# Threshold of eleven score steps moved from VectorE to GpSimd, in four instructions per step

## The chip, the cores and the metric

The kernel runs on one core of a Trainium2 chip. A core has five engines that run their own instruction lists side by side and meet through semaphores: TensorE (PE in the profile, with PEld for its weight loads), VectorE (DVE), ScalarE (ACT), GpSimd (POOL) and SyncE (SP, which here only issues DMAs). The metric is the device time of one execution in microseconds (us); lower is better. Before the change it is 442.55 us, the median of three runs from 441.95 to 442.66.

## What is computed

Eight batches of an attention with a threshold, followed by a gated MLP whose gate mixes the sequence positions. The part that the change touches is the second line of `_attn_ref`: only scores within `tau` (0.02) of the row's largest are kept.

```python
def _attn_ref(q, k, v, tau):                  # q, k, v: (8, 8, 576, 64) float32
    scores = (1.0 / np.sqrt(64)) * np.matmul(q, k.transpose(0, 1, 3, 2))
    thresh = np.max(scores, axis=-1, keepdims=True) - tau
    scores = np.where(scores >= thresh, scores, -1000000000.0)
    scores = scores - np.max(scores, axis=-1, keepdims=True)
    attn = np.exp(scores)
    attn = attn / (np.sum(attn, axis=-1, keepdims=True) + 1e-09)
    return np.matmul(attn, v)

def _moe_ref(x, w_in, w_spatial, b_spatial, w_out):   # x: attention, heads side by side
    h = np.maximum(x @ w_in, 0.0)
    u, v = h[..., :512], h[..., 512:]
    v_n = (v - mean(v)) / np.sqrt(var(v) + 1e-06)     # over the last axis
    v_s = np.einsum('ts,bsd->btd', w_spatial, v_n) + b_spatial[None, :, None]
    return (u * v_s) @ w_out
```

## The kernel before

**Steps.** The attention of one batch is cut into 18 score steps, 144 in all, numbered g = 18b + j. A step is 128 rows of scores of two heads: 128 x 2 x 576 values. `scores` and `scores_end` (the matmuls of line 712) fill one of two PSUM tiles, `s_ring[g % 2]`, so the matmuls of step g+2 wait until ScalarE has read step g out of its tile.

**Two ways to threshold.** `top` (line 746) takes each row's largest score on VectorE. Then a step goes one of two ways, by the table `ON_ACT`:

- On ScalarE (84 steps): `shift` (line 752, VectorE, 128 x 2) makes a bias, `spread` (line 761) subtracts it with a Prelu whose slope throws what is under the threshold to minus infinity, and `exps` (line 781) takes the exponential.
- Through VectorE (60 steps): `spread` (line 764) writes e = exp(score - largest) into one of three tiles, `e_ring[g % 3]`, one ScalarE instruction per head, and `mask` (line 776) makes the numerators p = (e >= ctau) * e in one VectorE instruction of 128 x 1152, where `ctau` is exp(-tau). Both of its tensor inputs are the same tile e in SBUF.

The numerators go to a `p_ring` tile in bfloat16, are transposed by DMA (tokens T) and multiplied with v (tokens P, p).

**The order of the work.** It is written out by hand: `ORDER` holds four lists of tokens, for batches 0, 1, 2 and 3 to 7, and `run_token` emits them one after another; each engine runs its instructions in that order. `name:d` means "of the batch d before this one" (d = -1: the next one). The tokens that matter here:

| token | what it emits | engine, line |
|---|---|---|
| S, Y | the score matmuls of a step, first and last part | PE, 712 |
| G | a GpSimd no-op between them (`turn_bank`): it waits until S has written the bank that both heads share, and Y waits for it | POOL, 727 |
| M (H, K by halves) | the largest of each row | DVE, 746 |
| B | the bias of a step on ScalarE | DVE, 752 |
| E, F | `spread` of head 0 and head 1 | ACT, 761 or 764 |
| Z / W | `exps` / `mask` | ACT, 781 / DVE, 776 |
| sq, sv | q and k, or v, of a pair of heads brought into another layout | POOL, 197 / 224 and 230 |
| QA, QB, QR and qa, qb, qr, kd | transposes of q, k and the last rows on PE, the copies out of PSUM on ACT, and a small copy on POOL (350) | PE, ACT, POOL |
| v, ev, bv, bs | a block of the MLP's v, its Relu (with row sums in ev), its statistics in bs | PE, ACT 554/557, DVE 565 |
| n, k, N | the mean from those sums (`mean`), the squares of v minus that mean (`square`), and the normalized v (`norm`) | POOL 570, ACT 576, POOL 583 to 595 |

A step that is masked by VectorE in batch j is listed as W in `ORDER`; in batches 3 to 7 these are steps 5, 6, 7, 8, 9, 11, 14 and 17. Around steps 7 and 11 the list for those batches reads:

```
F7 M8 v1 sv0 E7 ev0 W7 S9 T10 bv1 G9 Y9 E8 QR3 M9 v2 qr3 F8 kd3 o3 W8 E9 S10 ev2 G10 sq0:-1 TR0 eo3 Y10
P01 F9 M10 n0 P00 sv1 k0 L5:-1 S11 B10 p01 E10 G11 N0 ...
... v4 F11 M12 L2:-1 E11 u1 bv4 B12 W11 S13 eu1 G13 n3 T20 Y13 F12 N1 QR0:-1 M13 R0 qr0:-1 E12 QA0:-1 k2 r0
S14 G14 qa0:-1 B13 N2 bs4 Y14 F13 OUT3 P11 M14 E13 ...
```

In the compiled program the no-op of token G is an instruction of GpSimd's sequencer alone: it waits for a PE semaphore and raises one that PE waits for.

Of the kernel before, what the change touches and what calls it, by code (L numbers as in the profile page):

```python
# [15 lines left out]
ORDER = [(  # L16
    "L7:0 L8:0 S0:0 G0:0 Y0:0 Ci0:0 S1:0 M0:0 G1:0 Y1:0 QB1:0 L9:0 M1:0 F0:0 QA1:0 E0:0 B1:0 qb1:0 W0:0 "
    "S2:0 F1:0 G2:0 Y2:0 E1:0 QR1:0 M2:0 Z1:0 S3:0 G3:0 Y3:0 dqa1:0 E2:0 T00:0 M3:0 qr1:0 F2:0 kd1:0 "
    "sq2:0 S4:0 B3:0 W2:0 F3:0 G4:0 Y4:0 E3:0 Z3:0 M4:0 S5:0 Ci2:0 G5:0 Cis0:0 L3:-1 Y5:0 QR2:0 QA2:0 "
    "B4:0 Cb0:0 dqr2:0 sv2:0 F4:0 M5:0 QB2:0 E4:0 qb2:0 T01:0 dqa2:0 S6:0 F5:0 G6:0 sq3:0 Y6:0 E5:0 M6:0 "  # L20
    "Z4:0 S7:0 G7:0 kd2:0 Y7:0 sv0:0 B6:0 F6:0 RP00:0 M7:0 Ci3:0 RP01:0 Cis2:0 E6:0 Ci1:0 rp01:0 drp00:0 "
    "Z6:0 B7:0 W5:0 QR3:0 S8:0 G8:0 F7:0 sv3:0 Y8:0 T10:0 P00:0 E7:0 dqr3:0 M8:0 sv1:0 Z7:0 S9:0 G9:0 "
    "Y9:0 B8:0 p00:0 F8:0 QB3:0 M9:0 E8:0 R0:0 S10:0 L0:-1 B9:0 r0:0 G10:0 kd3:0 E9:0 Y10:0 Cs2:0 F9:0 "
    "M10:0 L4:-1 Z8:0 S11:0 G11:0 Cis3:0 Y11:0 qb3:0 T11:0 M11:0 E10:0 QA3:0 F10:0 B11:0 qa3:0 S12:0 "
    "E11:0 G12:0 Cis1:0 Y12:0 F11:0 M12:0 L1:-1 Z9:0 S13:0 L6:-1 G13:0 Cbs0:0 Y13:0 B12:0 Z11:0 W10:0 "
    "XR0:0 P10:0 QR0:-1 F12:0 M13:0 E12:0 T20:0 S14:0 dqr0:-1 B13:0 p10:0 G14:0 E13:0 Y14:0 P01:0 F13:0 "
    "M14:0 Z12:0 S15:0 sq0:-1 Cs1:0 p01:0 G15:0 F14:0 Y15:0 L5:-1 Css4:0 XP0:0 M15:0 E14:0 P11:0 Z13:0 "
    "kd0:-1 dxp0:0 p11:0 QA0:-1 T21:0 B15:0 F15:0 QB0:-1 S16:0 E15:0 dqb0:-1 G16:0 W14:0 qa0:-1 Y16:0 "
    "S17:0 Z15:0 G17:0 sq1:-1 Y17:0 M16:0 Cs0:0 P20:0 L7:-1 XP1:0 Css2:0 dxp1:0 L8:-1 B16:0 p20:0 E16:0 "
    "M17:0 Css3:0 F16:0 T30:0 P21:0 F17:0 p21:0 E17:0 Z16:0 L2:-1 L9:-1 "),  # L30
(
    "WS2:1 S0:0 dws2:1 G0:0 Y0:0 S1:0 M0:0 G1:0 Y1:0 QA1:0 M1:0 F0:0 RP11:1 qa1:0 rp11:1 W17:1 QB1:0 E0:0 "
    "RP10:1 F1:0 S2:0 W0:0 E1:0 G2:0 sq2:0 Y2:0 rp10:1 S3:0 M2:0 qb1:0 G3:0 Y3:0 T31:1 sq3:0 QR1:0 P30:1 "
    "B2:0 M3:0 qr1:0 F2:0 QA2:0 kd1:0 E2:0 W1:0 F3:0 S4:0 E3:0 G4:0 Y4:0 p30:1 Z2:0 S5:0 M4:0 Co0:1 G5:0 "
    "Css0:1 Y5:0 qa2:0 L1:-1 XP2:1 M5:0 xp2:1 QB2:0 sv1:0 qb2:0 QR2:0 qr2:0 B4:0 B5:0 R1:1 W3:0 F4:0 "
    "T00:0 P31:1 E4:0 E5:0 r1:1 S6:0 F5:0 G6:0 kd2:0 p31:1 Y6:0 Z4:0 M6:0 XP3:1 WS0:1 S7:0 L0:-1 ws0:1 "
    "G7:0 dxp3:1 Cos0:1 L4:-1 Y7:0 F6:0 Css1:1 v0:1 M7:0 E6:0 v1:1 bv0:1 W6:0 F7:0 v2:1 T01:0 E7:0 bs0:1 "
    "S8:0 bv1:1 G8:0 ev2:1 bs1:1 Y8:0 RP01:0 Z5:0 n2:1 M8:0 QB3:0 sv2:0 Co1:1 S9:0 qb3:0 G9:0 sv0:0 L5:-1 "
    "drp01:0 Y9:0 E8:0 v3:1 M9:0 XR1:1 F8:0 sq0:-1 RP00:0 bv3:1 S10:0 B9:0 drp00:0 E9:0 T10:0 G10:0 N0:1 "
    "W7:0 Y10:0 k2:1 u3:1 F9:0 M10:0 QA3:0 eu3:1 S11:0 qa3:0 G11:0 Y11:0 B10:0 L8:-1 W8:0 F10:0 sq1:-1 "  # L40
    "QR3:0 P00:0 L6:-1 qr3:0 E10:0 u1:1 p00:0 Z9:0 M11:0 S12:0 kd3:0 G12:0 eu1:1 Cos1:1 Y12:0 T11:0 N2:1 "
    "P01:0 E11:0 M12:0 v4:1 F11:0 B12:0 p01:0 S13:0 bv4:1 W11:0 G13:0 F12:0 Y13:0 Co2:1 u0:1 E12:0 L3:-1 "
    "M13:0 Z10:0 QB0:-1 S14:0 eu0:1 dqb0:-1 G14:0 sv3:0 Y14:0 Z12:0 bs3:1 R0:0 T20:0 N1:1 P11:0 B13:0 "
    "r0:0 F13:0 E13:0 p11:0 u4:1 H14:0 WS3:1 N3:1 eu4:1 ws3:1 QA0:-1 K14:0 L7:-1 WS1:1 B14:0 XR0:0 F14:0 "
    "S15:0 dws1:1 Cos2:1 bs4:1 G15:0 qa0:-1 Y15:0 E14:0 M15:0 QR0:-1 WS4:1 qr0:-1 Z14:0 S16:0 T21:0 G16:0 "
    "N4:1 Y16:0 B15:0 dws4:1 E15:0 XP0:0 u2:1 dxp0:0 F15:0 H16:0 P20:0 Z13:0 K16:0 S17:0 L9:-1 eu2:1 "
    "B16:0 G17:0 kd0:-1 p20:0 Y17:0 E16:0 TR1:0 P10:0 H17:0 Z15:0 s0:1 p10:0 K17:0 F16:0 es0:1 E17:0 "
    "P21:0 F17:0 p21:0 T30:0 Z16:0 Co3:1 L2:-1 "),
(
    "S0:0 G0:0 Y0:0 XP1:1 M0:0 QA1:0 xp1:1 S1:0 qa1:0 G1:0 B0:0 Y1:0 E0:0 QR1:0 M1:0 XP2:1 qr1:0 xp2:1 "  # L50
    "s1:2 F0:0 B1:0 W17:1 E1:0 QB1:0 F1:0 S2:0 G2:0 es1:2 qb1:0 T31:1 Y2:0 S3:0 Z0:0 M2:0 G3:0 kd1:0 Y3:0 "
    "sq2:0 s2:2 M3:0 E2:0 Cos3:2 QA2:0 F2:0 sq3:0 L1:-1 es2:2 F3:0 S4:0 L0:-1 W2:0 E3:0 G4:0 Y4:0 L8:-1 "
    "P30:1 qa2:0 M4:0 Z1:0 QB2:0 S5:0 qb2:0 p30:1 T00:0 G5:0 Y5:0 B4:0 W3:0 QR2:0 P31:1 qr2:0 E4:0 kd2:0 "
    "s3:2 F4:0 M5:0 Z4:0 S6:0 p31:1 G6:0 sv0:0 Y6:0 B5:0 es3:2 R1:1 F5:0 sq0:-1 M6:0 E5:0 o0:2 L5:-1 Z5:0 "
    "L6:-1 S7:0 r1:1 G7:0 Y7:0 eo0:2 B6:0 X1:1 o1:2 M7:0 F6:0 E6:0 o2:2 T01:0 deo1:2 E7:0 S8:0 deo2:2 "
    "F7:0 G8:0 sv3:0 Y8:0 Z6:0 S9:0 M8:0 G9:0 Y9:0 u2:1 TR0:0 W7:0 F8:0 v0:1 eu2:1 E8:0 L4:-1 M9:0 QA3:0 "
    "bv0:1 S10:0 qa3:0 G10:0 T10:0 B9:0 bs0:1 Y10:0 E9:0 QR3:0 o3:2 F9:0 dqr3:0 M10:0 s4:2 Z9:0 S11:0 "
    "es4:2 eo3:2 W8:0 G11:0 N0:1 L7:-1 Y11:0 F10:0 v1:1 OUT3:2 E10:0 M11:0 QB3:0 bv1:1 S12:0 qb3:0 G12:0 "
    "B11:0 bs1:1 Y12:0 E11:0 T11:0 sv1:0 v2:1 F11:0 M12:0 N1:1 v3:1 bv2:1 B12:0 u3:1 bs2:1 bv3:1 bs3:1 "
    "u1:1 kd3:0 eu3:1 Z11:0 W10:0 R0:0 OUT1:2 S13:0 L3:-1 eu1:1 r0:0 G13:0 sv2:0 E12:0 Y13:0 v4:1 M13:0 "  # L60
    "F12:0 S14:0 bv4:1 T20:0 B13:0 G14:0 sq1:-1 Y14:0 F13:0 P01:0 M14:0 N2:1 E13:0 P00:0 Z12:0 p01:0 "
    "S15:0 B14:0 G15:0 p00:0 L2:-1 Y15:0 F14:0 QR0:-1 M15:0 QB0:-1 qr0:-1 P10:0 qb0:-1 E14:0 B15:0 bs4:1 "
    "QA0:-1 Z13:0 S16:0 T21:0 p10:0 G16:0 kd0:-1 Y16:0 N3:1 dqa0:-1 F15:0 P20:0 M16:0 E15:0 u4:1 Z15:0 "
    "S17:0 p20:0 G17:0 N4:1 Y17:0 B16:0 OUT4:2 eu4:1 P11:0 Z14:0 TR1:0 u0:1 p11:0 E16:0 H17:0 s0:1 eu0:1 "
    "K17:0 F16:0 T30:0 P21:0 es0:1 F17:0 p21:0 E17:0 Z16:0 X0:0 L9:-1 "),
(
    "S0:0 G0:0 Y0:0 QA1:0 M0:0 QR1:0 S1:0 qr1:0 qa1:0 G1:0 kd1:0 B0:0 Y1:0 W17:1 E0:0 QB1:0 F0:0 s1:2 "
    "M1:0 qb1:0 Z0:0 S2:0 T31:1 G2:0 sq2:0 B1:0 Y2:0 es1:2 E1:0 s3:2 M2:0 F1:0 R1:1 B2:0 es3:2 F2:0 S3:0 "
    "r1:1 G3:0 E2:0 Y3:0 s2:2 L0:-1 Z1:0 M3:0 L3:-1 Z2:0 S4:0 es2:2 G4:0 B3:0 Y4:0 F3:0 o0:2 M4:0 E3:0 "
    "T00:0 P30:1 eo0:2 B4:0 S5:0 E4:0 p30:1 G5:0 F4:0 Y5:0 QA2:0 M5:0 Z3:0 P31:1 L4:-1 qa2:0 S6:0 p31:1 "  # L70
    "F5:0 G6:0 sq3:0 Y6:0 X1:1 E5:0 o1:2 M6:0 o2:2 eo1:2 T01:0 W5:0 F6:0 QB2:0 E6:0 S7:0 eo2:2 G7:0 W6:0 "
    "Y7:0 qb2:0 S8:0 Z4:0 G8:0 Y8:0 M7:0 L1:-1 QR2:0 s4:2 qr2:0 L8:-1 kd2:0 v0:1 sv2:0 es4:2 F7:0 M8:0 "
    "v1:1 sv0:0 E7:0 ev0:1 W7:0 S9:0 T10:0 bv1:1 G9:0 Y9:0 E8:0 QR3:0 M9:0 v2:1 qr3:0 F8:0 kd3:0 o3:2 "
    "W8:0 E9:0 S10:0 ev2:1 G10:0 sq0:-1 TR0:0 eo3:2 Y10:0 P01:0 F9:0 M10:0 n0:1 P00:0 sv1:0 k0:1 L5:-1 "
    "S11:0 B10:0 p01:0 E10:0 G11:0 N0:1 p00:0 Y11:0 F10:0 T11:0 QB3:0 M11:0 v3:1 qb3:0 Z10:0 n2:1 bs1:1 "
# [1048 lines left out]
```

## Time and profile before

| what | value |
|---|---|
| median of three runs | 442.55 us (441.95 to 442.66) |
| span of the profiled execution (first to last instruction) | 440.2 us |
| PE, DVE, ACT, POOL busy | 411.0, 394.3, 388.0, 178.7 us |
| `mask`, line 776 | 60 instructions, 85.5 us, mean 1427 ns |
| `top`, line 746, both heads at once | 135 instructions, 1352 to 1361 ns |
| `spread`, line 764, one head | 120 instructions, mean 749 ns |
| GpSimd `norm`, line 595, 128 x 512, float32 to bfloat16 | 28 instructions, mean 772 ns |
| GpSimd `mean`, line 570, 128 x 1 | 16 instructions, mean 440 ns (some 190 ns where nothing disturbs it) |
| granted TensorE clock | 0.999 |

A batch of the steady part takes some 51 us. Instruction rows in the timeline are given as start, duration, engine, line, operation, tiles; a bracket at the end is idle time of that engine before the instruction and what ended it. An engine's busy share is no more than a first hint: which wait ends last, stage by stage, tells what a change there is worth.

### The profile page before, as it was taken

What the parts mean: (1) busy time and instruction counts of PE and PEld (TensorE: products, weight loads), DVE (VectorE), ACT (ScalarE), POOL (GpSimd) and SP (SyncE); (2) the same over time, 40 slices, a digit from 0 to 9 for tenths busy, and PEclk for the clock granted to TensorE, in tenths of its full rate; (3) what the DMA queues carried; (4) which work ended last, traced back from release to release, by engine and by line L of the source; (5) the groups of instructions that cost most, each with busy time, mean ns of one, the idle gap of its engine ahead of it and who ended that gap; (6) DMA issues with size and microseconds to landing.
All of it is one profiled execution on the core that took longest, in us unless ns stands there. A gap on an engine that the chain in (4) does not pass through costs nothing.

```text
span 440.2 us, 12827 instructions
## 1 busy us (share of the span) xinstructions
PE 411.0 (93%) x4997; PEld 260.9 (59%) x5048; DVE 394.3 (90%) x641; ACT 388.0 (88%) x621; POOL 178.7 (41%) x383
## 2 busy tenths in 40 slices
PE   8677789999999999999999999999999999999995
PEld 4454556566555666666565666666566666565553
DVE  6997899998999898999999998999989998999782
ACT  3899799999899999999999989999899999999352
POOL 1445443860416511773146711574127711345021
PEclk9999999999999999999999999999999999999999
DMA  7999999899999999999999999999999998976913
GB/s 197 284 213 215 286 224 240 176 180 208 247 157 246 189 188 193 223 220 187 234 216 166 246 216 200 221 231 182 218 188 221 235 190 158 163 111 83 281 67 109
DMA packets 222620, 88.15 MB, mean 200 GB/s; under 512 B 193632, under 2 KB 218336, under 8 KB 222560
## 3 DMA queue, kind: packets, MB, share of 16 engines
q1 hardware_dynamic: 222032, 86.48, 95.0%
q8 instruction: 40, 0.66, 0.6%
q0 software_dynamic: 160, 0.52, 0.3%
q10 hardware_dynamic: 368, 0.33, 0.2%
q14 instruction: 20, 0.16, 0.1%
HBM read 32.79 MB, written 9.44 MB: 96 GB/s over the span
## 4 chain that ended last, share of the span: by engine, by line
DVE 36%; PE 35%; ACT 18%; issue 8%; DMA 1%; POOL 0%; POOLq 0%; DVEq 0%; ACTq 0%
PE s L712 14%; DVE s L746 13%; DVE p L776 9%; DVE negm L746 6%; ACT e L761 6%; ACT e L764 4%; ACT p L781 4%; PE f L610 3%; PE f L668 3%; PE f L397 2%; PE f L639 2%; DVE xn L406 2%; PE f L338 2%; DVE st L565 2%; PE f L545 2%
## 5 line engine op out<-in xcount | busy, mean ns | idle before, releaser
L712 PE MATMUL s<-qkT 64*64 64x160 f32 (+1 forms) x2304 | 171.8, 415 | 13.5 <-ACT e L761 7.3
L712 PEld LDWEIGHTS s<-qkT 64*64 64x64 f32 x2304 | 106.7, 132 | 68.4 <-ACT e L761 17.4
L761 ACT ACTIVATE e<-s,negm 128x576 f32<-128x576 f32 x168 | 117.2, 744 | 12.1 <-DVE negm L752 6.5
L746 DVE TENSOR_REDUCE s<-s 128x2 f32<-128x1152 f32 (+1 forms) x91 | 115.3, 1268 | 10.8 <-PE s L712 9.3
L764 ACT ACTIVATE e<-s,negm 128x576 f32<-128x576 f32 x120 | 84.8, 749 | 9.4 <-DVE negm L746 8.1
L746 DVE TENSOR_REDUCE negm<-s 128x2 f32<-128x1152 f32 (+1 forms) x62 | 81.2, 1313 | 8.8 <-PE s L712 8.5
L776 DVE SCALAR_TENSOR_TENSOR p<-e,ctau 128x1152 bf16<-128x1152 f32 x60 | 85.5, 1427 | 1.3 <-ACT e L764 1.2
L781 ACT ACTIVATE p<-e 128x1152 bf16<-128x1152 f32 x68 | 79.0, 1171 | 0.4
L197 POOL COPY qn<-ql 128x512 f32<-128x512 f32 x31 | 25.5, 821 | 81.1 <-PE s L712 80.7
L397 PE MATMUL f<-v,pT 128*128 128x65 bf16 x1008 | 44.5, 194 | 0.0
L397 PEld LDWEIGHTS <-pT 128*128 128x128 bf16 x1024 | 41.4, 97 | 3.5 <-issue 1.8
L350 POOL COPY qkT<-qkT 64x64 f32<-64x64 f32 x32 | 7.9, 247 | 85.3 <-PE s L712 42.4
L406 DVE TENSOR_TENSOR xn<-f,r 128x256 bf16<-128x256 f32 (+1 forms) x93 | 35.4, 380 | 2.9
L639 PE MATMUL f<-wsT,vn 128*128 128x512 bf16 x117 | 32.6, 380 | 1.4 <-ACT qkT L320 0.4
L610 PE MATMUL f<-xT,w_in 128*128 128x512 bf16 x111 | 29.4, 381 | 0.5
L392 PE MATMUL f<-v,pT 128*128 128x130 bf16 x126 | 27.7, 220 | 1.1 <-DVE xT L314 0.7
L595 POOL TENSOR_SCALAR vn<-vrel,rs,nm 128x512 bf16<-128x512 f32 (+1 forms) x35 | 27.0, 770 | 3.6
L320 ACT COPY qkT<-f 128x512 f32<-128x512 f32 (+1 forms) x56 | 24.5, 439 | 3.4 <-PE f L357 3.2
L545 PE MATMUL f<-w_in,xT 128*128 128x512 bf16 x99 | 26.8, 379 | 0.8
L668 PE MATMUL f<-w_o,gT 128*128 128x512 bf16 x92 | 24.2, 380 | 0.4
L224 POOL CAST v<-vl 128x512 bf16<-128x512 f32 x32 | 20.0, 625 | 10.3 <-PE s L712 9.4
L230 POOL CAST v<-vx 64x64 bf16<-64x64 f32 x64 | 20.8, 326 | 1.9
(166 smaller groups left out, 570.9 us busy)
## 6 DMA issues: line engine op xcount, KB each, us to landing
vl<-in_v_dram SPq DMA_DIRECT2D x16, 512.0 KB, 4.7
ql<-in_q_dram SPq DMA_DIRECT2D x15, 512.0 KB, 5.0
kl<-in_k_dram SPq DMA_DIRECT2D x15, 512.0 KB, 5.3
out_dram<-oo SPq DMA_DIRECT2D x12, 512.0 KB, 5.0
uT<-in_moe_w_in_dram SPq DMA_DIRECT2D x3, 512.0 KB, 4.8
uT<-in_moe_w_spatial_dram SPq DMA_DIRECT2D x2, 576.0 KB, 4.6
pT<-p SPq DMA_TRANSPOSE x65, 6.3
vx<-in_v_dram SPq DMA_DIRECT2D x16, 64.0 KB, 3.7
```

The source lines that it names most:

```text
L397: nc.tensor.matmul(out=t[:, at + 65 * h:at + 65 * h + 65], lhsT=pt[:, 5 * h + j, :], rhs=vt[:, 6 * h + j, :], start=False, stop=(h == 1 an ...
L406: nc.vector.tensor_tensor(out=dst, in0=o[ps, g0:g1, 0:64], in1=r[ps, g0:g1].unsqueeze(2).broadcast_to([ps.stop - ps.start, g1 - g0, 64]), ...
L545: nc.tensor.matmul(out=t, lhsT=x_of(b, f, slice(c * P, (c + 1) * P)), rhs=w_in[:, f, 512:1024], start=(f == 0), stop=(f == 3))
L610: nc.tensor.matmul(out=t, lhsT=w_in[:, m, f * P:(f + 1) * P], rhs=x_of(b, m, slice(0, 512)), start=(m == 0), stop=(m == 3))
L639: nc.tensor.matmul(out=t, lhsT=vn[:, c, f * P:(f + 1) * P], rhs=wsT[:, c, 0:512], start=(c == 0), stop=(c == 4))
L668: nc.tensor.matmul(out=t[:n], lhsT=gs[b][:, f, c * P:c * P + n], rhs=w_o[:, f, :], start=(f == 0), stop=(f == 3))
L712: made.append(nc.tensor.matmul(out=s_ring[g % 2][halves[k], at[h] + lo:at[h] + hi], lhsT=qks[n][halves[h], 0, m:m + 64], rhs=qks[n][halves ...
L746: nc.vector.tensor_reduce(out=nm[:, heads], in_=view(s_ring[g % 2], at[h0], dims), axis=AX.X, op=ALU.max, negate=True)
L761: nc.scalar.activation(out=e, in_=s, func=ACT.Prelu, bias=bias_, scale=scale if steps[g][1] == 4 else 1.0, alpha=1e30)
L764: nc.scalar.activation(out=e, in_=s, func=ACT.Exp, bias=bias_)
L776: nc.vector.scalar_tensor_tensor(out=numerators(g), in0=ef, scalar=ctau, in1=ef, op0=ALU.is_ge, op1=ALU.mult)
L781: nc.scalar.activation(out=numerators(g), in_=e_ring[g % 3].rearrange("p h s -> p (h s)"), func=ACT.Exp)
```

## The change

In eleven steps (step 7 of batch 2, steps 7 and 11 of batches 3 to 7) the one VectorE instruction of `mask` is replaced by four GpSimd instructions. Per head, a comparison writes a mask of ones and zeros in bfloat16 into a new tile of its own (128 x 576), and a product of e and that mask writes the numerators. The table `ON_ACT` becomes `WAYS`, a letter per step: `a` for on ScalarE, `w` for `mask` as before, `s` for the new way. The other letters (`n`, `q`) are in the code but in no entry of the table, so `half_step` and `half_e` have no effect here. All other steps keep their way.

```diff
+WAYS = [
+    "wawaawaaaawaaawaaw",
+    "wwawaawwwaawaaaaaw",
+    "aawwaaaswawaaaaaaw",
+    "aaaaawwswwasaawaaw",
+]
...
+    kept_head = [const.tile([P, S], t, name=f"kept{h}")
+                 for h, t in enumerate((BF16, BF16))]
...
+    def keep_head(g, h):
+
+        nc.gpsimd.tensor_scalar(out=kept_head[h], in0=e_ring[g % 3][:, h, :],
+                                scalar1=ctau, scalar2=None, op0=ALU.is_ge)
+
+    def mask_head(g, h):
+
+        nc.gpsimd.tensor_tensor(out=numerators(g)[:, S * h:S * h + S], in0=e_ring[g % 3][:, h, :],
+                                in1=kept_head[h], op=ALU.mult)
...
+    stepwise = {"B": "anq", "Z": "a", "W": "wnq", "I": "sq", "J": "s", "U": "s", "V": "s"}
...
-        if kind in ("B", "Z", "W") and on_act(g) == (kind == "W"):
+        if kind in stepwise and way(g) not in stepwise[kind]:
             return
...
+             "I": lambda g: keep(g) if way(g) == "q" else keep_head(g, 0), "J": lambda g: keep_head(g, 1),
+             "U": lambda g: mask_head(g, 0), "V": lambda g: mask_head(g, 1)}[kind](g)
```

In `ORDER` the token W of these steps becomes four: I and J (the comparisons) stand where W stood, U and V (the products) come later, each behind a token G. The lists are otherwise the same, token for token; they are only wrapped at another width.

```
batch 2, step 7
-  G9 Y9 u2 TR0 W7 F8 v0 eu2 E8 ... S10 qa3 G10 T10 B9
+  G9 Y9 u2 TR0 I7 J7 U7 F8 v0 eu2 E8 ... S10 qa3 G10 V7 T10 B9
batches 3 to 7, step 7
-  E7 ev0 W7 S9 T10 bv1 G9 Y9 ... S10 ev2 G10 sq0:-1 TR0
+  E7 ev0 I7 J7 S9 T10 bv1 G9 U7 Y9 ... S10 ev2 G10 V7 sq0:-1 TR0
batches 3 to 7, step 11
-  bv4 B12 W11 S13 eu1 G13 n3 T20 ... S14 G14 qa0:-1 B13 N2
+  bv4 B12 I11 J11 S13 eu1 G13 U11 n3 T20 ... S14 G14 V11 qa0:-1 B13 N2
```

Counted in the built programs, VectorE loses 11 instructions of line 776 and GpSimd gains 22 comparisons and 22 products; PE, ACT and SP keep their instructions and their order.

## The prediction

> **What bounds the kernel now.** I read the page's busy shares and chain first, then the groups by shape for prices, then the steady part in stretches, and last the timeline around a removed instruction.
>
> ```profile
> PE 411.0 (93%) x4997; PEld 260.9 (59%) x5048; DVE 394.3 (90%) x641; ACT 388.0 (88%) x621; POOL 178.7 (41%) x383
> ...
> DVE 36%; PE 35%; ACT 18%; issue 8%; DMA 1%; POOL 0%; POOLq 0%; DVEq 0%; ACTq 0%
> ```
>
> Three engines are near 90%, and GpSimd, idle for more than half the time, is nowhere on the chain. That invites the change. But a share is a mean; batch 3 in stretches says who sets the pace where:
>
> ```profile
> core 0: us, PE busy (x) PEld busy (x) DVE busy (x) ACT busy (x) POOL busy (x), PEclk, DMA share, GB/s
> 178.00:184.00 6.00, 5.88 (x79) 3.51 (x77) 5.61 (x5) 5.69 (x13) 4.07 (x8) 1.00 1.25 259
> 184.00:196.00 12.00, 11.94 (x161) 7.86 (x162) 11.60 (x21) 11.94 (x24) 9.00 (x19) 1.00 0.93 207
> ```
>
> From 184 to 196 us ScalarE is busy for 11.94 of 12 us, and GpSimd for 9.0: just here it is not idle. Steps 7 and 11 lie at 178 and 190. The timeline around step 7:
>
> ```profile
> 178.52 1.41 DVE L776 SCALAR_TENSOR_TENSOR p<-e,ctau 128x1152 bf16<-128x1152 f32 x1
> ...
> 178.61 1.71 POOL L230 CAST v<-vx 64x64 bf16<-64x64 f32 x2
> ...
> 179.84 1.35 DVE L746 TENSOR_REDUCE negm<-s 128x2 f32<-128x1152 f32 x1
> ...
> 183.53 0.18 POOL L570 TENSOR_SCALAR nmean<-sm 128x1 f32<-128x1 f32 x1
> ...
> 183.74 0.72 ACT L576 ACTIVATE sq<-vrel,nmean 128x512 bf16<-128x512 f32 x1
> ...
> 186.58 0.42 PEld L338 LDWEIGHTS f<-identf,qn 128*128 128x128 f32 x4 [0.30 <-ACT qkT L320]
> ```
>
> Three things are to be seen. The mask of step 7 (178.52) lies beside the matmuls of step 9 (another row of the timeline, 178.53 to 179.73), so the next reduction (179.84) waited for PE as much as for the mask. On GpSimd two copies and a mean of row sums run from 182.38 to 183.71, and ScalarE's square, which needs that mean, starts 0.03 us after it, at 183.74, when ScalarE has just come free (183.67). And behind the square ScalarE has no gap, while PE already waits for it (the copy L320) at 186.58.
>
> **Removed.** Eleven instructions of 1.41 us, 15.5 us of VectorE time; what counts is how much earlier the next reduction can start. Step 7, batches 3 to 7: step 9's scores end at 179.73 and a reduction starts some 0.06 behind them (step 10: 182.85 to 182.91), so 179.79 for 179.84: 0.05. Step 11: its mask runs 190.44 to 191.85 and the next reduction starts at 191.77, while the scores end at 191.46: 0.25. Batch 2: the mask is at 126.91, the next reduction at 128.25, and its scores are done at 126.58, so it can come 1.40 earlier; but the spread that follows (129.89) stands behind a ScalarE copy that ends at 129.79, so 0.15 are left.
>
> **Added: prices.** No row has these operations at this size.
>
> ```profile
> L595 POOL TENSOR_SCALAR vn<-vrel,rs,nm 128x512 bf16<-128x512 f32 x28 | 21.6, 772 | 2.9
> ...
> L224 POOL CAST v<-vl 128x512 bf16<-128x512 f32 x32 | 20.0, 625 | 10.3 <-PE s L712 9.4
> ...
> L244 POOL CAST w_in<-uT 128x1024 bf16<-128x1024 f32 x3 | 3.1, 1040 | 5.3 <-PE s L712 5.3
> ...
> L586 POOL TENSOR_SCALAR rs<-ss 128x1 f32<-128x1 f32 x16 | 3.1, 192 | 4.6 <-ACT pr L781 2.2 <-PE s L712 1.3
> ```
>
> Comparison: L595 is the same kind (float32 to bfloat16, per-partition scalar). 0.19 fixed (L586) and 0.58 for 511 more columns give 0.19 + 0.65 = 0.845 us at 576. Ends: 0.67 (a cast: 0.62 at 512, and 0.42 for 512 more) and 1.04 (the cast of 1024). Product: it reads two inputs. Not under 0.845 (one input) and not over 1.69 (two passes). It reads 2 x 576 elements: L244 extended from 1024 to 1152 gives 1.15, and with the 1.25 by which L595 exceeds a cast of its size, 1.43; I take 1.3. A step thus puts 2 x 0.845 + 2 x 1.3 = 4.3 us on GpSimd for 1.4 taken from VectorE.
>
> [...]
>
> [...] The 64 x 64 cast at 178.61 took 1.41 us instead of 0.23 and ended at 180.02, just after the mask (179.93); in the trace every GpSimd read that overlaps a mask is held so (0.95 us for a mean of 0.19, ending at 191.90 behind a mask ending at 191.85). The other way the mask is held less: one that started 0.55 us before the end of a GpSimd copy (15.60; copy to 16.15) took 1.76, one 0.31 before (87.05) took 1.51, against 1.41. So a mask loses its overlap less some 0.2. L595, which has all kinds of VectorE work beside it, shows no hold by anything but masks: its 28 rows at 128 x 512 all take 771 to 774 ns.
>
> [...]
>
> **Step 7, batches 3 to 6**, in the times of batch 3. Without the mask the cast pair at 178.61 needs 0.53 (the pair at 184.21): to 179.14. Then I 179.22 to 180.07, J to 180.87 (instructions with no wait between them overlap by 0.05, as the two copies do), U 180.82 to 182.12. The mask of step 8 comes at 181.06 into U, loses 1.06 - 0.2 and runs to 183.3; the next reduction slips by 0.3, which is covered by what follows. The small copy (L350) is held by that mask to 183.4. V (allowed since the G at 182.18) runs 183.47 to 184.77, then the two copies, in the queue behind V, to 185.9, the mean to 186.05. The square waits for it: 186.08 instead of 183.74, **2.34 us late**. Behind it ScalarE's queue is full to 196 us: the spreads of step 10 (184.57), the copy at 185.95 for which PE waits at 186.58, and so the scores of step 12 and its reduction. I see no cover, so I count all of it: 4 x 2.34 = 9.4 us. Even with nothing before it late, V alone stands between G10 and the copies: 182.28 + 0.845 + 1.33 is 184.45, 0.7 late.
>
> **Step 7, batch 7.** No next batch, so no two copies: V to 184.77, mean to 184.9, square at 184.94 and the next spread 0.83 later, 185.77 against 184.57: 1.2 us. **Batch 2** has no mean here, and GpSimd is idle from 126.0 to 132.5: the four end by 130.9. Gain 0.15.
>
> **Step 11, five times.** I waits for the spread that ends at 189.92: 190.02 to 190.87, J to 191.66, U to 192.91, a mean to 193.07, the normalization's four instructions (2.15 from mean to end in the trace, 191.90 to 194.05) to 195.22, V 195.17 to 196.47. Spread F14 writes the same e tile (14 and 11 are equal modulo 3) and now must wait for V: 196.54 against 196.34. So 0.2 lost, 5 x 0.2 = 1.0, and the 0.25 of VectorE is not used.
>
> **G.** A sequencer no-op does not wait for the instruction in execution: the one at 150.78 ended inside an L595 that ran 150.26 to 151.03, and at 179.07 one ended while a cast was held to 180.02. So G costs nothing; I waits only for spreads that S waits for too. **DMAs:** T11 now waits for V, 184.8, against its issue at 184.18; its consumer P11 runs at 195. Nothing. SP's later issues slip by 0.6, with microseconds to spare.
>
> **Sum:** 9.4 + 1.2 + 1.0 - 0.15 = +11.4 us. The profiled execution has a span of 440.2, the median is 2.35 above it; I add to the median: 453.9 (span 451.6).
>
> **Ends.** Low: 0.67 and 0.845, hardly a held mask: the square is 1.1 late (4.3 in all), batch 7 nothing, step 11 gains 0.25 x 5, batch 2 up to 1.4: +1.7, 444.2. High: 1.04 and 1.69: the mask of step 8 gets the port before U, V ends at 186.3, the square is 3.9 late (15.6), batch 7 2.8, step 11 1.4 x 5 = 6.9: +25, 467.8.
>
> **Rivals.**
> (a) Faster: VectorE sets the pace. For it: 36% of the chain. Place: the reductions behind the removed masks; price: all that they can move, 1.4 + 5 x 0.05 + 5 x 0.25 = 2.9 us, 439.6. It decides only where the mean comes before ScalarE is free (183.67): copies and mean take 1.33 of the 1.5 us from G10 on, so V would have to fit in 0.2, while the cheapest row says 0.845. Or ScalarE's delay would have to be made up later; its first gaps over 0.2 come at 207. 10%.
> (b) Cheap products, the low end: 443.5 to 447, 9%.
> (c) Dear ones, masks and GpSimd blocking each other in turn: 461 to 469, 8%.
> (d) The no-ops stick behind a full GpSimd queue: G9 then waits for J (180.87 for 179.07), G13 for J (0.9), G14 for the normalization (1.6), so PE stalls 4.3 us more in each of five batches: some 475. The two no-ops above speak against it. 4%.
> (e) The losses and gains cancel: 3%.
> That the change does less than it says is excluded by the instruction counts.
>
> My forecast (447 to 461) has 66%. About 0.2% (0.9 us) is what a measurement of this kernel can tell from no change: faster 10%, same 3%, slower 87%. The range from 443.5 to 464 leaves out (a), (d), (e) and part of (c), 2 in 10.
>
> **What would show it.** On the profile after: a wait of several microseconds of ACT L590 (the square) for POOL in batches 3 to 6, four times over 1.5 us; products between 1.1 and 1.5 us and comparisons near 0.85; masks of step 8 of some 2.2 us; the copies qn, kn directly behind V; F14 waiting for POOL; no wait of PE on the no-op's line. I am wrong if the square doesn't wait, or if it waits and the batches are no longer: then ScalarE was not what set the end there.

## The result, and the profile after

The changed kernel takes 475.35 us (median of four runs, 473.59 to 476.89) against 442.61 us for the kernel before in the same comparison: a ratio of 1.073, 95% interval 1.069 to 1.076. The forecast was 453.9 us, the range 443.5 to 464. The direction was right; the loss is 32.7 us where 11.4 were forecast, and the time lies outside the range. The profiled execution took 474.39 us, span 472.6.

The first page of the profile after, busy shares and the shares of the chain that ended last:

```profile
span 472.6 us, 12892 instructions
...
PE 426.1 (90%) x4997; PEld 263.9 (56%) x5048; DVE 383.2 (81%) x630; ACT 387.7 (82%) x621; POOL 234.4 (50%) x427
...
PE 35%; DVE 22%; ACT 20%; issue 11%; POOL 9%; DMA 1%; POOLq 0%; DVEq 0%; ACTq 0%
```

GpSimd, at 0% of the chain before, is now on 9% of it. VectorE and ScalarE have fallen from 90 and 88% busy to 81 and 82%, PE from 93 to 90%. The same two stretches of batch 3 as before the change show where:

```profile
core 0: us, PE busy (x) PEld busy (x) DVE busy (x) ACT busy (x) POOL busy (x), PEclk, DMA share, GB/s
178.00:184.00 6.00, 4.75 (x39) 2.00 (x37) 3.50 (x3) 5.46 (x12) 5.80 (x6) 1.00 1.22 258
184.00:196.00 12.00, 11.31 (x134) 6.73 (x135) 8.85 (x14) 9.03 (x18) 10.54 (x17) 1.00 0.85 163
```

From 178 to 184 us it is GpSimd that is full (5.80 of 6), and PE is busy for 4.75 instead of 5.88. The groups by shape give the prices that the prediction had to bound:

```profile
L822 POOL TENSOR_SCALAR kept<-e,ctau 128x576 bf16<-128x576 f32 x22 | 37.8, 1724 | 4.3 <-ACT e L793 3.7
L827 POOL TENSOR_TENSOR p<-e,kept 128x576 bf16<-128x576 f32 x22 | 28.6, 1303 | 0.4
```

A product takes 1.30 us, as taken. A comparison takes 1.72, twice what was taken (0.845) and above the upper end (1.04). The waits (engine and line that waited, for whom; us in total, times, longest):

```profile
PEld s L732 <- POOLq L747: 33.4, 24, 2.9
...
PE s L732 <- POOLq L747: 18.7, 15, 2.2
...
ACT sq L590 <- POOL nmean L584: 15.0, 5, 3.2
```

The third row is what the prediction named: the square (L590) waits for the mean, 3.2 us instead of 2.3. The first two are what it excluded: PE waits for the no-op of the G tokens (L747). PEld and PE wait at the same time; PE's wait is shorter (1.21 against 1.93 us at G10 of batch 3, in the timeline below), as its matmuls run to 182.86 and its weight loads end at 182.14. In the kernel before, the first row (there L712 and L727) was 1.8 us in all:

```profile
PEld s L712 <- POOLq L727: 1.8, 4, 0.8
```

The timeline of batch 3 after the change, around steps 7 and 11:

```profile
179.17 3.43 POOL L822 TENSOR_SCALAR kept<-e,ctau 128x576 bf16<-128x576 f32 x2
...
182.57 1.39 POOL L827 TENSOR_TENSOR p<-e,kept 128x576 bf16<-128x576 f32 x1
...
184.02 0.23 POOL L364 COPY qkT<-qkT 64x64 f32<-64x64 f32 x1
184.07 0.19 PEld L732 LDWEIGHTS s<-qkT 64*64 64x64 f32 x4 [1.93 <-POOLq L747]
184.07 0.49 PE L732 MATMUL s<-qkT 64*64 64x160 f32 x4 [1.21 <-POOLq L747]
184.34 1.28 POOL L827 TENSOR_TENSOR p<-e,kept 128x576 bf16<-128x576 f32 x1
...
186.92 0.72 ACT L590 ACTIVATE sq<-vrel,nmean 128x512 bf16<-128x512 f32 x1 [3.21 <-POOL nmean L584]
...
192.96 3.44 POOL L822 TENSOR_SCALAR kept<-e,ctau 128x576 bf16<-128x576 f32 x2 [0.30 <-ACT e L793]
...
196.36 1.28 POOL L827 TENSOR_TENSOR p<-e,kept 128x576 bf16<-128x576 f32 x1
...
198.83 0.26 POOL L604 TENSOR_SCALAR nm<-mv,rs 128x1 f32<-128x1 f32 x1
...
199.20 0.20 PEld L732 LDWEIGHTS s<-qkT 64*64 64x64 f32 x4 [2.72 <-POOLq L747]
199.20 0.76 POOL L609 TENSOR_SCALAR vn<-vrel,rs,nm 128x512 bf16<-128x512 f32 x1
```

The no-ops are instructions of GpSimd's sequencer (POOLq L747, 17 ns each); the trace has them at 184.00 (G10) and 199.14 (G14), each between two neighbours of this list. G10 comes 0.04 us after U7 ends (183.96) and just before the small copy kd3 (L364), which stands ahead of it in GpSimd's order. G14 comes 0.05 after `nm` (L604) ends (199.09), just before the last instruction of the normalization N1, also ahead of it. The copy kd3 had its data from ScalarE since 180.39. But the trace also has it wait for the semaphore that GpSimd's own instructions raise, and it began when U7 had ended. (The value that it waits for is not kept; that it is U7's is read from the times.) So each no-op came when the last instruction ahead of it had its wait met, not when an engine had free time.

How late a step is tells more than the total. For each kernel I took the start of a step's first score matmul, counted from the start of its batch, less the same in the kernel before. "PE held" is how much later the weights of token Y are loaded behind those of token S than in the kernel before; where it is over 0.5 us the no-op is listed (in e9_free11 the only one). Batch 4, in us, is like batches 5 and 6 to within 0.4:

| kernel | PE held at the no-op | step 12 late | next batch late |
|---|---|---|---|
| changed kernel | G10 1.79, G11 1.12, G14 2.58, G15 0.93 | 3.02 | 6.22 |
| e1_only7 | G10 1.79, G11 1.11 | 3.00 | 2.78 |
| e2_only11 | G14 2.62 | 0.00 | 3.59 |
| e5_madd (comparison at 0.82) | G11 1.89, G14 0.77, G15 0.95 | 2.12 | 3.55 |
| e6_mean | G10 1.86, G11 0.96 | 2.81 | 2.77 |
| e7_copies | none | 3.43 | 4.38 |
| e8_both | none | 0.61 | 3.49 |
| e10_step7 | G13 1.20 | 0.57 | 1.39 |
| e9_free11 | G16 0.33 | 0.00 | 0.60 |

Batches 0 and 1 have none of the change, and batch 2 is 0.1 shorter. Batch 0 alone varies from 44.9 to 49.6 us between these profiles, so differences of a microsecond are read from the later batches.

### The profile page after: what moved, and what is told of

It reads as the page before. It is cut to its first block, busy times and chain, and to the rows that moved or that the text cites. A ratio compares the mean times of both kernels' runs of the same rounds, so it can differ in the third digit from the quotient of the medians.

```text
span 472.6 us, 12892 instructions
## 1 busy us (share of the span) xinstructions
PE 426.1 (90%) x4997; PEld 263.9 (56%) x5048; DVE 383.2 (81%) x630; ACT 387.7 (82%) x621; POOL 234.4 (50%) x427
## 4 chain that ended last, share of the span: by engine, by line
PE 35%; DVE 22%; ACT 20%; issue 11%; POOL 9%; DMA 1%; POOLq 0%; DVEq 0%; ACTq 0%
PE s L732 15%; DVE s L766 10%; ACT e L790 6%; DVE p L811 4%; ACT p L832 4%; PE f L411 4%; PE f L624 3%; ACT e L793 3%; POOL p L827 3%; PE f L352 3%; DVE negm L766 2%; PE f L682 2%; POOL v L238 2%; PE f L559 1%; ACT qkT L334 1%
## 5 line engine op out<-in xcount | busy, mean ns | idle before, releaser
L732 PE MATMUL s<-qkT 64*64 64x160 f32 (+1 forms) x2304 | 184.1, 422 | 31.6 <-POOLq L747 18.7
L811 DVE SCALAR_TENSOR_TENSOR p<-e,ctau 128x1152 bf16<-128x1152 f32 x49 | 71.0, 1450 | 1.2 <-ACT e L793 1.2
L211 POOL COPY qn<-ql 128x512 f32<-128x512 f32 x31 | 24.4, 786 | 72.9 <-PE s L732 72.4
L364 POOL COPY qkT<-qkT 64x64 f32<-64x64 f32 x32 | 7.9, 246 | 83.5 <-PE s L732 40.8
L411 PE MATMUL f<-v,pT 128*128 128x65 bf16 x1008 | 47.4, 199 | 0.0
L411 PEld LDWEIGHTS <-pT 128*128 128x128 bf16 x1024 | 44.2, 101 | 2.7 <-issue 0.2
L822 POOL TENSOR_SCALAR kept<-e,ctau 128x576 bf16<-128x576 f32 x22 | 37.8, 1724 | 4.3 <-ACT e L793 3.7
L827 POOL TENSOR_TENSOR p<-e,kept 128x576 bf16<-128x576 f32 x22 | 28.6, 1303 | 0.4
```

What stands on the lines that cost most here:

```text
L411: nc.tensor.matmul(out=t[:, at + 65 * h:at + 65 * h + 65], lhsT=pt[:, 5 * h + j, :], rhs=vt[:, 6 * h + j, :], start=False, stop=(h == 1 an ...
L732: made.append(nc.tensor.matmul(out=s_ring[g % 2][halves[k], at[h] + lo:at[h] + hi], lhsT=qks[n][halves[h], 0, m:m + 64], rhs=qks[n][halves ...
L811: nc.vector.scalar_tensor_tensor(out=numerators(g), in0=ef, scalar=ctau, in1=ef, op0=ALU.is_ge, op1=ALU.mult)
L822: nc.gpsimd.tensor_scalar(out=kept_head[h], in0=e_ring[g % 3][:, h, :], scalar1=ctau, scalar2=None, op0=ALU.is_ge)
L827: nc.gpsimd.tensor_tensor(out=numerators(g)[:, S * h:S * h + S], in0=e_ring[g % 3][:, h, :], in1=kept_head[h], op=ALU.mult)
```

## The experiments

All times are medians; each ratio is against runs of the kernel before on the same chip (442.35 to 443.61 us). Three theories run through what was expected: (1) PE stands because the no-ops of the G tokens are held up; (2) the square's wait for the mean sets the delay, as predicted; (3) the price of the comparison drives the loss.

### One step alone

```diff
 e1_only7                                  e2_only11
-"aaaaawwswwasaawaaw",                     -"aawwaaaswawaaaaaaw",  -"aaaaawwswwasaawaaw",
+"aaaaawwswwawaawaaw",                     +"aawwaaawwawaaaaaaw",  +"aaaaawwwwwasaawaaw",
-B12 I11 J11 S13 eu1 G13 U11 n3            -E7 ev0 I7 J7 S9 T10 bv1 G9 U7
+B12 W11 S13 eu1 G13 n3                    +E7 ev0 W7 S9 T10 bv1 G9
```

> Only step 7 of batches 2 to 7 stays on GpSimd; step 11 is VectorE's mask again. Theory 1 (the no-ops of the G tokens are held up behind GpSimd instructions whose wait is not met, and PE stands with them): batches 3 to 6 each lose what G10 and G11 lost in the changed kernel (1.79 + 1.11, 3.0 us at the scores of step 12), batch 7 loses 1.9, the second half of each batch keeps its old length: about +13.8, 456.4 us, with PE's wait for the no-op unchanged at G10 and G11. Theory 2 (the prediction: the square's wait for the mean sets the delay, the no-ops cost nothing): 3.2 us of square in four batches and some 2 in batch 7: also +14 to +15; so the time alone does not part the two, but by theory 2 PE's idle time would be named after ScalarE's copy, not after GpSimd's sequencer. If step 11 costs nothing of its own, the time stays near 475.

> Only step 11 of batches 3 to 7 stays on GpSimd. Theory 1: G14 stands behind a normalization whose four instructions wait for one another and for the comparisons ahead of them, so each of five batches loses some 3.3 us from step 14 on: about +16.5, 459 us, with a wait of PE for the no-op of G14 of over 2 us in each batch and no lateness before step 13. Theory 2 (the prediction's own term for step 11): spread F14 waits for V11, 5 x 0.2 = +1, 443.6 us.

e1_only7: 455.92 us, 1.029 (1.024 to 1.034). e2_only11: 461.47, 1.042 (1.036 to 1.048). The two losses, 13.1 and 18.6, add up to 31.7 of 32.7, so there is little that only the two steps together cost. Step 11, costed by the prediction at 1 us, is the dearer one, and its loss begins at G14, not at spread F14. For step 7 both theories expected the same, so it stayed open.

### What a comparison costs, and what a no-op waits for

```diff
 e3_mult, in keep_head
-                                scalar1=ctau, scalar2=None, op0=ALU.is_ge)
+                                scalar1=ctau, scalar2=None, op0=ALU.mult)
 e4_probe, in the kernel before, behind token G2 (x0, x1, yy: scratch)
+        if it == 3:
+            for t in yy:
+                ts(out=t, in0=x0, scalar1=ctau, scalar2=None, op0=ALU.is_ge)
+        elif it == 4:
+            for a, c in ((x0, x1), (x1, x0), (x0, x1), (x1, x0)):
+                ts(out=c, in0=a, scalar1=ctau, scalar2=None, op0=ALU.is_ge)
...
+            ts(out=yy[0], in0=x0, scalar1=ctau, scalar2=None, op0=ALU.mult)
+            ts(out=yy[1], in0=x0, scalar1=ctau, scalar2=ctau, op0=ALU.mult, op1=ALU.add)
```

> The comparison of the 22 GpSimd instructions becomes a multiplication with the same scalar: the same count, tiles, waits and order; the threshold is left out in those eleven steps. Theory 3 (the price of the comparison drives the loss): the multiplication takes about 0.85 us against 1.72; then U7 ends near 182.2, G10 is not held, the square is still some 2.3 us late, and G14 waits for the normalization about 0.8: 4 x 2.3 + 1.2 + 5 x 0.8 = some +14.5, 457 us. Rival (the price belongs to this form with one operation and a scalar from a tile, whichever operation): 1.7 us again and 475 us.

> The kernel before, with scratch instructions on GpSimd behind token G2 in four batches, their results unused. Prices at 128 x 576 from float32: comparison to bfloat16 1.72; multiplication 0.85, multiplication and addition 0.85 (rival: one operation costs as much as a comparison); comparison with a constant 1.72, comparison and multiplication in one 1.7 or more; product float32 x bfloat16 1.28, float32 x float32 1.3; maximum between 0.85 and 1.72. For the no-op: batch 3 has four comparisons that are independent of one another, 6.9 us of work in front of G3, which comes 2.9 us after G2. Theory 1: none of the four has an unmet wait, G3 passes and the scores of step 3 are on time (under 0.4 late). Theory 4 (a limit on what may be queued or executing ahead of a no-op): G3 comes some 4 us late. Batch 4 has four comparisons each reading what the one before wrote: theory 1 has G3 held until the third ends, 3 x 1.72 = 5.2 us after the start, some 2.3 us late; if a no-op passes waiting instructions too, it is on time.

e3_mult: 474.78 us, 1.071 (1.065 to 1.077): no gain. My expectation fell and its rival held. The probe says why; its lines 183, 184 and 190 are a multiplication, a multiplication with an addition, and a maximum (count, then shortest, median and longest in ns, when, shape):

```profile
L183 POOL TENSOR_SCALAR wsb<-x,ctau x1: 1734/1734/1734, 264.6 to 264.6; 128x576 bf16<-128x576 f32 x1
...
L184 POOL TENSOR_SCALAR wsb<-x,ctau x1: 817/817/817, 266.3 to 266.3; 128x576 bf16<-128x576 f32 x1
...
L190 POOL TENSOR_SCALAR y<-x,ctau x1: 1727/1727/1727, 317.8 to 317.8; 128x576 bf16<-128x576 f32 x1
```

One operation with a scalar from a tile took 1.72 to 1.73 in all three that were tried (comparison, multiplication, maximum); the pair of multiplication and addition took 0.82. The probe has a single instruction of each but the comparison. The comparison with a constant took 1.65, comparison and multiplication in one instruction 2.21, the products 1.28 and 1.40. The row L595 from which the prediction had its price is a multiplication with an addition, the one cheap form among those tried.

For the no-op, PE's rows of batches 3 and 4 (step 3 at 163.24 and at 213.78):

```profile
163.24 1.20 PE L737 MATMUL s<-qkT 64*64 64x160 f32 x16
...
213.78 1.19 PE L737 MATMUL s<-qkT 64*64 64x160 f32 x12
217.13 0.49 PE L737 MATMUL s<-qkT 64*64 64x160 f32 x4 [2.17 <-POOLq L752]
```

In batch 3, with four independent comparisons in front of it (161.01 to 167.85), the no-op came at 163.77, while the second was in execution and two were still to come, and all 16 matmuls of the step ran through. In batch 4, with four that read one another's results, it came at 217.06, 0.06 after the fourth had started (217.00): 2.75 us late, as theory 1 had it (2.3). So in the probe work that was queued or in execution did not hold a no-op, and an instruction ahead of it with an unmet wait did.

### The price that the prediction took

```diff
 e5_madd, in keep_head
-                                scalar1=ctau, scalar2=None, op0=ALU.is_ge)
+                                scalar1=ctau, scalar2=ctau, op0=ALU.mult, op1=ALU.add)
```

> The changed kernel, with the comparison of the 22 GpSimd instructions replaced by a multiplication and an addition, the one form that took 0.82 us in the probe; threshold left out in those eleven steps. It gives the comparison the price that the prediction took (0.845). Theory 3 (the price drives the loss): U7 ends at 182.1 in the times of the kernel before, in time for G10; the square is some 2.3 us late in four batches and G14 waits some 0.6 for the normalization in five: 4 x 2.3 + 1.2 + 5 x 0.6 = +13, some 456 us, at most 460. If PE's waits for the no-op at G10 stay at 1.7 and the time over 468, the price is not what drives it.

459.68 us, 1.039 (1.034 to 1.044), just inside the limit that I had set. The instructions of line 822 now take 0.825 us. This splits the error of the forecast: 15.7 us (475.35 less 459.68) are the price of the comparison, the remaining 5.8 (459.68 less 453.9) something that the sum did not have. By batches, step 7 now loses 4 x 2.12 + 1.02 in batch 7 + 0.31 in batch 2 = 9.8, where the prediction's terms were 10.45. Step 11 loses 1.4 a batch, some 7.1, where its term was 1.0: the no-ops G14 to G16 behind the normalizations. The two parts are not independent. From these 9.8 and 7.1 to the 13.1 and 18.6 of the steps alone, the price adds 3.3 at step 7 and 11.5 at step 11, and at step 11 it acts through the no-op G14, held 2.6 instead of 0.8. Nor does this run tell what costs the 9.8, since beside the square the no-op G11 is held 1.89.

### Step 7: the square, or the no-ops?

```diff
 e6_mean    n0 moved:   E7 ev0 n0 I7 J7 S9 ...  (was behind M10)
 e7_copies  kd3, sv1:   ... S10 ev2 G10 kd3 V7 sq0:-1 ... S11 B10 p01 E10 G11 sv1 N0
 e8_both    as e6 and e7, and N0 behind G12
 e10_step7  as e8, but N0 behind G11, and sq0:-1 sv1 behind G12
```

> Step 7 alone on GpSimd as in e1_only7 (455.9 us), with one token moved: the mean n0 ahead of the comparisons, so the square no longer waits for GpSimd. Theory 2 (the square sets the delay, the no-ops cost nothing): nearly all of the 13 us go, some 444 to 446. Theory 1 (the no-ops set it): PE still stands 1.7 at G10 and 1.1 at G11, 455 to 456, no gain. If both paths are about equally late, also no gain, and e7_copies shows none either.

> Step 7 alone on GpSimd as in e1_only7 (455.9 us), with two tokens moved: the small copy kd3 behind G10 and the casts sv1 behind G11, so that no instruction with an unmet wait stands before these no-ops; the mean stays behind V7 and the square waits for it. Theory 1: PE's waits at G10 and G11 go, and with them the loss, some 444 to 446. Theory 2: the square still waits some 3 us and holds ScalarE's queue, so step 12 stays 2.3 to 3 late: 453 to 456. If either move alone brings nothing, and the two together (with N0 placed well) bring 10, the two waits lie side by side.

> Only step 7 on GpSimd, at the full price of the comparison, but in another order: the mean n0 ahead of the comparisons, the small copy kd3 behind G10, the casts sv1 behind G11, the normalization N0 behind G12, so that neither the square nor a no-op stands behind the products. Theories 1 and 2 together (those two waits are all of the loss): the 13 us of the kernel with step 7 alone go, but for step 10's second spread, which waits some 0.35 for V7: 443 to 446 us, and PE's waits for the no-op at G10 and G11 under 0.2. If GpSimd's load itself were the cause (port, masks, later chains), it stays above 450.

> Step 7 alone on GpSimd, at the full price, with both moves of e8_both and the one thing that it left late: there the normalization N0 came behind five copies and held a buffer that ScalarE waited for (0.9 to 2.1 us, and after 1.8 us without PE work the granted clock fell to 0.5 for some 3.4 us). Now N0 stands right behind G11, the copies sq0 and the casts sv1 behind G12. Theories 1 and 2: what is left is some 0.4 per batch of step 10's second spread waiting for V7, five times 0.4 to 0.6: 444 to 446 us. If GpSimd's load in the stretch as such were the limit, some engine waits for another late GpSimd result and the time stays over 450.

From 455.92 for step 7 alone: e6_mean 456.67 us, 1.031 (1.027 to 1.034); e7_copies 460.46, 1.040 (1.036 to 1.043); e8_both 457.01, 1.032 (1.027 to 1.037); e10_step7 448.63, 1.013 (1.009 to 1.016). e7_copies (453 to 456 expected at most) and e10_step7 (444 to 446 if the two waits were all) came out above that. In e6_mean the square's wait is gone from the table of waits and PE's remains; in e7_copies it is the other way round (one row of e6_mean, then two of e7_copies):

```profile
PEld s L728 <- POOLq L743: 16.3, 13, 2.0
...
ACT sq L586 <- POOL nmean L580: 15.1, 5, 3.2
...
PEld s L728 <- POOLq L743: 2.0, 4, 1.1
```

Step 12 is 2.8 late with the no-ops' waits alone (e6_mean), 3.0 to 3.5 with the square's alone (e7_copies), 3.0 with both (e1_only7) and 0.6 with neither (e8_both, e10_step7). So the two waits lie side by side, either is enough to make step 12 as late, and a kernel that mends one shows no gain. That e8_both is no faster either has a cause of its own behind step 12:

```profile
ACT vrel L567 <- POOL vn L605: 7.7, 5, 2.1
```

I had moved N0 so far back that ScalarE waited for the buffer that N0 reads. With N0 put forward (e10_step7) this row is gone. What is left there is some 0.4 for step 10's second spread, which waits for V7, and 1.2 at G13, behind the casts sv1: the instructions put back ended up in front of another no-op.

### Step 11 in another order

```diff
 e9_free11: N1 behind G12; N2 behind G15; kd0:-1 sv3 sq1:-1 behind G17
```

> Only step 11 on GpSimd, at the full price, in another order: the normalization N1 ahead of the comparisons behind G12, N2 behind G15, and the copies sq1, sv3 and kd0 behind G17. Theory 1: no instruction with an unmet wait stands before G14 any more; of the 18.6 us of the kernel with step 11 alone at most 3 are left (V11 ends some 0.2 after spread F14 wants its tile): 442 to 446 us. If the loss is GpSimd's load in this stretch, over 452.

446.41 us, 1.009 (1.006 to 1.012): at the full price of the comparison, all but 4.0 of the 18.6 us are gone, and of PE's waits at the no-ops 0.33 at G16 is left per batch. For step 11 theory 1 is shown.

### Both steps in another order, and the most that there was to gain

```diff
 e13_whole:  sv0 sv1 behind sq3; J7 I7 n0 behind ev0; kd3 behind G10; N0 behind G11;
             sq0:-1 behind n2; N1 behind G12; N2 behind G15; N4 N3 behind G16; kd0:-1 sq1:-1 sv3 behind G17
 e11_nomask: I7 J7 U7 V7 (batches 2 to 7) and I11 J11 U11 V11 taken out of the lists
 c1_step6:   steps 7 and 11 as W; batches 3 to 7: J6 behind G7, I6 behind G8, V6 U6 behind kd2;
             sv0 behind sq3, sv2 behind U6
 c2_step6:   as c1_step6, but n0 kd3 behind G10, N0 behind G11, sv1 sv2 behind G12
 e14_no6:    as c1_step6 without J6 I6 V6 U6, sv0 and sv2 in their old places
```

> The whole change, both steps, every GpSimd instruction at its full price, in a repaired order: the casts sv0 and sv1 moved up behind sq3, where GpSimd is idle; J7, I7, then the mean n0; kd3 behind G10, N0 behind G11, sq0 behind n2, N1 behind G12, N2 behind G15, N4 and N3 behind G16, kd0, sq1 and sv3 behind G17. If order (what stands before which no-op, and the square's mean) is all of the 32 us: what is left is V11, 0.2 to 0.5 late for spread F14, and half-met waits of that size, 443 to 447 us. If GpSimd is simply overfull between 179 and 203 us (its work there grows by 12 us per batch), new waits of over 1 us per batch appear: 450 to 460.

> The most that the change could have given: the eleven masks are left out and nothing is put in their place, so the numerators of those steps are not made (what the transposes read there is left over from earlier steps); all else as in the changed kernel. The prediction's gains: 0.15 in batch 2, 5 x (0.05 + 0.25) behind it: 440.9 us. The prediction's rival that VectorE sets the pace: 439.6. If the masks lie entirely beside other work: 442.5, no change.

> Steps 7 and 11 on VectorE as before; in batches 3 to 7 step 6 goes to GpSimd instead, where it was idle from 171.9 to 176.6 us: J6 behind G7, I6 behind G8, V6 and U6 behind kd2, sv0 moved up behind sq3, sv2 behind U6. In the kernel before, the mask of step 6 (174.32 to 175.73) keeps the reduction of step 7 from starting when its scores end (174.8), and ScalarE idles 0.63 before 177.10 for that reduction. If these waits are what a removed mask can give: 5 x 0.6 = 3 us less, some 439.6. Rival: the products beside the masks of steps 7 and 8 cost as much again: 442 to 446.

> As c1_step6 (step 6 of batches 3 to 7 on GpSimd instead of steps 7 and 11), with no instruction that waits in front of G9, G10, G12: sv0 behind sq3, n0 and kd3 behind G10, N0 behind G11, sv1 and sv2 behind G12. In c1_step6 PE stood 3.6 us at G9 behind the second small cast of sv2. If that was all, the 31 us go, and what the missing mask gives is seen: there the scores of step 9 came 0.2 earlier, 5 x 0.2 = 1 us, 441.4; otherwise 443 to 446 through the masks of steps 7 and 8, which run beside the products.

> The most that could be had from step 6: its mask is left out in batches 3 to 7 and nothing is put in its place (the numerators of that step are left over from earlier steps); all other steps on VectorE or ScalarE as before. Reading the profile of before: the reduction of step 7 starts 0.8 earlier, ScalarE's idle 0.63 goes: up to 5 x 0.6 = 3 us, 439.4; by what c1_step6 showed at step 9, 5 x 0.2, 441.4.

e13_whole: 457.37 us, 1.031 (1.027 to 1.035). Order gives back some 18 of the 32 us. The rest is what the rival said: PE is held 0.6 at G7, 0.3 at G13 and 1.4 at G17, and a square waits 1.3 for its mean: the 12 us more work per batch (four comparisons and four products) did not fit between the no-ops in this order. Whether another order would do better is open.

e11_nomask: 442.20 us, 0.999 (0.996 to 1.001). With the masks gone and nothing in their place, the kernel is no faster within the interval; batches 3 to 7 are shorter by 0.1 to 0.2 each but for one that is 0.2 longer. So the change had at most 1.7 us to win (the interval's end), and by the batches under 1. The rival that VectorE sets the pace, 439.6, lies below the interval and falls; the gain of 1.65 that the prediction's terms give is not told from none.

c1_step6 was a miss: 473.31 us, 1.069 (1.065 to 1.073). I had looked at GpSimd's idle time and not at what stood before G9: the second small cast of sv2 waits there for the large one ahead of it, and PE stood 3.6 us. c2_step6, with that mended, is 452.46, 1.019 (1.016 to 1.021), still above both expectations: step 9 comes 0.2 earlier, as e14_no6 has it, and then G13 is 1.5 late behind sv1 and sv2. e14_no6 itself: 442.08, 0.998 (0.996 to 1.001), which can't be told from no change; batches 3 to 7 are 0.06 to 0.19 shorter. No version that does the threshold beats the kernel before.

### What a stall costs beside itself

In e7_copies batch 3 ends 2.83 us late and batches 4 to 6 end 4.38, 4.26 and 4.19 late, with the same waits. The difference is in the granted clock, here of the changed kernel behind G14 of batch 3 (stretch, its length, then busy time of PE, PEld, DVE, ACT and POOL; the clock follows the last bracket):

```profile
core 0: us, PE busy (x) PEld busy (x) DVE busy (x) ACT busy (x) POOL busy (x), PEclk, DMA share, GB/s
197.00:199.00 2.00, 0.21 (x2) 0.00 (x0) 0.74 (x2) 2.00 (x5) 1.73 (x5) 1.00 0.93 227
199.00:200.00 1.00, 0.80 (x14) 0.57 (x15) 0.19 (x1) 0.12 (x2) 0.89 (x3) 1.00 1.07 381
200.00:201.00 1.00, 1.00 (x27) 1.00 (x24) 1.00 (x1) 0.00 (x0) 1.00 (x1) 0.69 0.10 29
201.00:203.00 2.00, 2.00 (x22) 1.41 (x22) 1.20 (x5) 1.74 (x3) 1.64 (x5) 0.50 0.04 8
203.00:204.00 1.00, 1.00 (x21) 0.56 (x16) 0.29 (x1) 1.00 (x3) 0.83 (x3) 0.60 0.00 0
204.00:205.00 1.00, 0.95 (x13) 0.53 (x11) 1.00 (x3) 0.74 (x1) 0.80 (x3) 1.00 0.71 134
```

PE was without work from 197.21 to 199.20, and from about 200.4 to 203.8 it was granted half its clock. This costs some 1.5 us in e7_copies; in the changed kernel the batches with such a spell (3, 5 and 6) end 6.4 to 6.6 late and batch 4, without one, 6.2. It is not the main part of the loss: with e5_madd, whose clock stays at 0.999, 17 us are lost all the same.

Not every gap in PE's work cost clock: gaps of 1.8 to 2.2 us were followed by half the clock in 15 of 20 cases of these runs (in the changed kernel, with gaps of 2.00 to 2.16, in 4 of 5).

Which of the gaps can be told from the traces. Within a run the slow spells start whole multiples of 3.413 us apart: in the changed kernel at 200.38, 313.02, 371.05 and 425.66, with 112.64, 58.03 and 54.61 us between them, which are 33, 17 and 16 of them. I cut every run, from 5 to 430 us, into stretches on this grid. The clock was halved behind all 26 stretches in which PE was without a matmul for 1.80 us or more in sum, and behind none with less than 1.74 (two of four between); in the changed kernel behind the four with 1.90 to 2.23 us, and behind none of the others, with 1.57 at most. So the gap of 2.73 us in batch 3 of e7_copies, which the grid cuts into 1.6 and 1.1, cost no clock, and the same gap in batches 4 to 6, with 2.3 to 2.7 in one stretch, did.

## Why the prediction was right or wrong

- **What bounds the kernel: right.** VectorE's masks are beside the path (e11_nomask), ScalarE's queue from 184 to 196 us has no cover (in e7_copies the square is 3.2 late and step 12 at least 3.0), and GpSimd is not idle just there. The 0.25 a batch that step 11 could give did not show: with no masks at all (e11_nomask), steps 12 to 15 of batches 3 to 6 start within 0.02 of the kernel before.
- **Price of the comparison: the term that was mis-sized, 0.845 for 1.72.** "L595 is the same kind" was the step: it is the same in its types and its scalar, but it is a multiplication with an addition, and in the probe that pair took 0.82 where the multiplication alone took 1.73. The upper end came from a cast and so missed it too. Worth 15.7 of the 21.4 us of error, most of it through the no-op at G14 (below).
- **Product: right**, 1.30 for 1.3.
- **The square's wait: right in mechanism**, four times over 1.5 us as listed, 3.2 instead of 2.34; at the price taken (e5_madd) it is 2.3, and step 7 loses 9.8 for 10.45 forecast. That the sum fits is partly luck: the held no-ops lie beside this wait and were not in it, and they alone would make step 12 nearly as late (e6_mean).
- **"G costs nothing": wrong.** With the price, it is the step that failed, and in step 11 it is most of the loss: PE waits 2.6 us for G14 in each batch (e2_only11), and with nothing unmet ahead of G14 all but 4.0 of 18.6 us go (e9_free11). Both no-ops that spoke for it, at 150.78 and 179.07, did end inside a GpSimd instruction, but all instructions ahead of them had already been released. They showed that execution did not hold these two, and I took them to show that the queue does not hold a no-op. Rival (d) named the place and its time (475) came true, partly by luck: its mechanism, a full queue, is not the one (e4_probe, batch 3), and it was worked out with the low price. At that price (e5_madd) the kernel takes 5.8 us more than the sum, where rival (d) had some 21, and G9, which it named first, is held 0.13 at most.
- **Held masks: too high.** The mask of step 8 took 1.68, not 2.2: it met the comparison, not a product, and beside the comparison, with 1.45 us of overlap, it lost 0.27. The port that the prediction's high end gives to this mask shows in no run; what shows is time lost where the two overlap: these 0.27, and in the kernel before a cast of 1.41 for 0.23 beside a mask (178.61). Nor is every read of GpSimd held, as the prediction has it: the copy at 182.38 in the kernel before overlaps a mask by 0.14 and takes its usual 0.61.
- **F14 waiting for V11** was to be 0.2. With G14 held, F14 is late for another reason: the reduction that it needs ends at 201.17, beside V11 (201.22), so the term adds next to nothing. In e9_free11, where nothing else is late, the wait is there: 0.4.
- **Batch 2: right**, 0.13 for 0.15.

## What to carry to other kernels

A synchronizing no-op on GpSimd was here only as quick as the last unmet wait ahead of it (2.75 us late in the probe). Before work is put on an engine that has such no-ops, list for each of them which instructions ahead of it depend on one another. Take a price only from a row with the same operations, not just the same types and shape, and try an instruction alone where no row has it. And before a mask, or any work, is moved off a busy engine, run the kernel with it left out: here that one run says that there were at most 1.7 us to gain.

## What the runs showed of the hardware that was not expected

- On GpSimd, at 128 x 576 from float32, one operation with a scalar from a tile took 1.72 to 1.73 us (comparison, multiplication, maximum), multiplication with addition 0.82, comparison with multiplication 2.21.
- A no-op of GpSimd's sequencer passed instructions that were released and queued (in the probe at 163.77, with two of four comparisons still to come), and was held behind one whose wait was unmet (2.75 us in the probe; at G14 of the changed kernel PE's weight loads stood 2.72 to 2.88 us).
- After gaps of 1.8 to 2.2 us in PE's work the granted clock fell to 0.5 for 3.4 us or twice that, in 15 of 20 cases; after gaps of 1.0 to 1.3 us never. On a grid of 3.413 us it was halved behind all 26 stretches with 1.80 us or more of the gap in them, and behind none with less than 1.74.
